# Earlier part closes, fewer expert steps in a B stage and more in a sort's end: one planner's order of a convolution with experts

## The chip, the cores and the metric

The kernel runs on one core of a Trainium2 chip. A core has TensorE (PE, with its weight loads shown as PEld), VectorE (DVE), ScalarE (ACT), GpSimd (POOL) and SyncE (SP), which issues the transfers. The time is device microseconds of one execution. Smaller is better.

## The reference

Two pieces follow each other. A long convolution along the sequence, through a Fourier transform of doubled length, and on its rows a layer of eight experts, of which each row uses the one with the highest logit:

```
x (8, 5696, 128), h (5696, 128)
Y = irfft(rfft(x, 2S) * rfft(h, 2S), 2S)[:, :S, :]        # S = 5696
r = Y.reshape(45568, 128)
logits = r @ w_gate                                        # (45568, 8)
e = argmax(logits);  gate = softmax(logits)[e]
out = gate * (relu(r @ w1[e]) @ w2[e])                     # w1 (8,128,1024), w2 (8,1024,128)
```

All of it is float32, and the output holds every row at its own place.

## The kernel before, in words

The doubled length is 2 x 48 x 119, so a transform goes in two factors. The eight batches are cut into groups of 2, 3 and 3 (`SPLIT`), numbered 0, 1 and 2, and each group passes three stages.

*Stage A* is the 119-point transform. Blocks of x are loaded (`xt`), split into two fp32r halves (`xc`, ScalarE L272 and another engine), multiplied (`pa`, L294), copied out (`ut`) and stored to `U` in DRAM (L287). For groups 1 and 2 it is a *guest* in the sort of the group before: `Guest.begin` puts two `pa` steps into each half-slot of that sort.

*Stage B* runs over the 120 frequencies of the first factor; an *item* is one of them for all batches of the group (in groups 1 and 2). An item is one 48-point product `xp` (L503, reads `uq`, loaded from `U` four frequencies at a time at L447, and `mt`), three multiplications with the filter's spectrum `hh` on VectorE (L515, L520, L522), a sum on GpSimd (L530), the inverse `vp` (L539) and a copy to `vt`, which is stored to `V` (L589).

*Stage C*, called the sort, takes `vq` back from `V`, makes the inverse 119-point product `yp` (L705), turns the rows (`tp`, L173), forms logits (`tp`, L746), counts rows by expert (`gb`, L770 and L771), works out every row's place, and GpSimd scatters each row to its expert's region of `SR` (L628). A slot is a pass over a few positions of all batches of the group: 16 slots in group 0 and 24 in groups 1 and 2, each of two half-slots, and each half-slot ends in a `yield`. When the slot named in `HALVES` is reached, a *part* closes: `tables` works out on VectorE (its last operations are the chain that ends at L948) which expert each tile of 256 rows belongs to, and after the last scatter of the part its rows may be loaded (`xr`, L1042).

*The experts.* 185 tiles of at most 256 rows are planned, cut by the parts into runs, and 182 of them are always computed. A tile is turned (`mx`, L173), passes layer 1 in four half-units (`mh`, L1091, six fp32r matmuls each), relu on ScalarE and VectorE (L1097, L1099), layer 2 in four half-units (`ma`, L1112), is copied (`ot`, L1122), turned back, scaled (`xr`, L1130) and scattered to the output (L1167). Weights come from `WD` in four pieces of 512 KB (`wb`, L1062); where the next tile has the same expert the load is skipped. Tiles done while a sort still scatters are staged in DRAM and scattered later.

*The order.* Each engine runs its instructions in the order written, SP's and GpSimd's queues too. That order comes from `run`: streams (the B and C stages in turn, the preparation of weights, the experts) are generators that yield a planned duration, and the stream with the least planned time goes next. An expert step is `STEP` = 1420 and holds one half-unit of layer 1 and one of layer 2. A B item of group 1 yields `STEP * MIX_B[1]` = 0.45 of a step, a half-slot of the sort `STEP * MIX_C[g]`, and half of that when all synthesis steps are done. `state["alone"]` is true while no part is ready; then no expert step goes beside the sort. `usable` lets a tile's rows be loaded `SETTLED` planned ns after the part's last scatter. After a sort's last half-slot the planner calls `next(after)`, which runs the next B stage's first loads.

Of the kernel before, what the change touches and what calls it, by code (L numbers as in the profile page):

```python
# [43 lines left out]
HALVES = ((12,), (8, 24), (24,))  # L44
STEP = 1420
MIX_A = (0.0, 0.45, 0.8)
MIX_B = (0.0, 0.45, 0.85)
MIX_C = (1.0, 1.2, 2.2)
STAGED = 64
# [3 lines left out]
HOLD = 3  # L53
GUESTED = (0,)
SETTLED = (2840, 8000, 8000)
# [12 lines left out]
def conv_moe(ctx: ExitStack, tc: tile.TileContext, I, out, B, S, D, E, F, split):  # L68
# [39 lines left out]
    class Part:  # L108
        def __init__(self, s, upto, tiles):
            self.s, self.upto, self.nt = s, upto, tiles  # L110
            self.sorted = self.tabled = self.filled = False
            self.lanes, self.fills = [], []
            self.since = 0
# [315 lines left out]
    def phase_b(gr, guest=None):  # L429
# [131 lines left out]
        N = len(items)  # L561
# [12 lines left out]
        for n in range(N + ds_ + 2 + HOLD):  # L574
# [28 lines left out]
            if n == N - 4 and g in GUESTED and guest:  # L603
                guest.fetch()
# [9 lines left out]
    state |= {"alone": True, "prepped": False, "defer": False, "spare": False, "now": 0}  # L614
# [43 lines left out]
    def phase_c(gr, guest=None, after=None):  # L658
# [9 lines left out]
        nu = NB // NI  # L668
# [194 lines left out]
        for k in range(AHEAD):  # L863
            divide(*divmod(k, nsub))
        TL, LL = TURN[g], LOGIT[g]
# [3 lines left out]
        for n in range(n_end + 1):  # L869
            for k in range(nsub):  # L870
# [17 lines left out]
                yield cost if n < nu else cost / 2  # L888
                if guest:
                    guest.end()  # L890
                if n < nu:
                    divide(*divmod(at + AHEAD, nsub))
                    settle(n, k)
# [19 lines left out]
        if guest:  # L913
            yield from guest.rest()
            state["spare"] = g > 0
        state["alone"] = False
        more = True
        while more or sorts:
            left = len(sorts)
            chore(3)  # L920
            more = after is not None and next(after, None)
            yield more or STEP
            if not more and len(sorts) == left:
                sort_one()
            if not sorts:
                state["defer"] = False
        chore(99)

    def tables(pt, base):
# [72 lines left out]
        pt.tabled = True  # L1002
# [179 lines left out]

    def usable(t):
        pt = seq[t][0]
        return pt.ready and state["prepped"] and not state["alone"] and state["now"] >= pt.since + SETTLED[min(pt.s, 2)]

    def pipeline(lo, hi):
# [3 lines left out]
        while True:  # L1191
            t, k = step
            while nw[0] < min(t + 3, hi) and seq[nw[0]][0].tabled and state["prepped"]:
# [18 lines left out]
            if act is None and old is None and to is None and ti is None:  # L1212
                leave(len(hist))
# [9 lines left out]
            if act:  # L1223
                layer1(t, k)
                passed[t, 0] = k
# [153 lines left out]
```

## Time and profile before

Three runs took 2313.42 to 2324.03 us, with a median of 2319.02 us.

| what | us |
|---|---|
| profiled execution, its own time | 2319.18 |
| its span | 2317.0 |
| TensorE busy | 2115.6 (91% of the span) |
| VectorE busy | 1556.2 (67%) |
| ScalarE busy | 1098.8 (47%) |
| GpSimd busy | 1193.0 (51%) |
| mean granted clock of TensorE | 0.966 |

Rows of the trace begin with the start in us from the beginning of the span, then the busy time of the row, the engine, the line of the code and the operation; out<-in are the program's names, and the bracket holds the idle time before it and what ended it ("issue": nothing that the profile shows). `SPq` is SP's own queue of transfers. A line by stretches gives, for each engine, its busy us and the number of instructions. A tile with name `xp`, `yp` or `mh` says which stage an instruction belongs to.

### The profile page before, as it was taken

Reading aid. Unit: us, or ns where it says so; the run is one execution under the profiler, and the core shown is the slowest. Engines: PE = TensorE matmul, PEld = TensorE weight load, DVE = VectorE, ACT = ScalarE, POOL = GpSimd, SP = SyncE. Lnnn points to the kernel's source line nnn. Section 1 sums busy time; section 2 is a strip of 40 time slices with the busy share of each in tenths; the row PEclk is TensorE's granted clock in tenths of the full one; section 3 lists DMA queues with packets and bytes.
Section 4 is the critical chain, followed back from the end, with each engine's and each line's share of the span. In section 5 each row is a group of like instructions: output and inputs, shape, how many; then the busy total and the mean of one; then the engine's idle time right before and its main releaser. Section 6 shows DMA issues by size and latency. Waiting matters only on the chain. (4 is left out here: it accounts for less than half of the span.)

```text
span 2317.0 us, 46736 instructions
## 1 busy us (share of the span) xinstructions
PE 2115.6 (91%) x14190; PEld 1776.5 (77%) x14190; DVE 1556.2 (67%) x3755; ACT 1098.8 (47%) x2359; POOL 1193.0 (51%) x1230
## 2 busy tenths in 40 slices
PE   7899787699997998978999999989879999999997
PEld 5688554366666887866777679878779999999997
DVE  4588644489996677768988785667565455555554
ACT  4688544233333665633434345556434444444443
POOL 5366337656653266752556561656554444444432
PEclk9999999799999999989999999999999999999998
DMA  9899998399997788857889877666645344444430
GB/s 294 272 323 319 317 341 236 118 262 284 268 276 217 204 257 255 235 160 214 235 243 261 225 234 212 191 176 194 176 130 157 129 136 138 137 137 136 140 116 28
DMA packets 254776, 485.47 MB, mean 210 GB/s; under 512 B 33221, under 2 KB 154690, under 8 KB 254523
## 3 DMA queue, kind: packets, MB, share of 16 engines
q1 hardware_dynamic: 230587, 435.36, 63.5%
q0 software_dynamic: 23936, 47.09, 6.6%
q8 instruction: 115, 1.88, 0.3%
q14 instruction: 138, 1.13, 0.2%
HBM read 592.96 MB, written 173.25 MB: 331 GB/s over the span
## 5 line engine op out<-in xcount | busy, mean ns | idle before, releaser
L1099 DVE SCALAR_TENSOR_TENSOR hs<-mh,hs 128x512 fp32r<-128x512 f32 x728 | 501.6, 690 | 451.7 <-ACT hs L1097 380.1
L1091 PE MATMUL mh<-xtb,wb 128*128 128x256 f32 x4368 | 708.5, 298 | 52.7 <-DMA wb<-WD 25.2
L1097 ACT ACTIVATE hs<-mh 128x512 fp32r<-128x512 f32 x728 | 434.5, 598 | 541.0 <-PE mh L1091 431.6
L1091 PEld LDWEIGHTS mh<-xtb,wb 128*128 128x128 f32 x4368 | 596.4, 193 | 122.4 <-issue 62.7
L1112 PE MATMUL ma<-hs,wb 128*128 128x256 f32 x4368 | 661.8, 288 | 7.5 <-DMA wb<-WD 5.7
L628 POOL DMA_INDIRECT SR<-rt,pi x384 | 404.2, 1053 | 380.1 <-ACT hs L1097 120.6
L1112 PEld LDWEIGHTS ma<-hs,wb 128*128 128x128 f32 x4368 | 580.6, 193 | 9.2 <-DMA wb<-WD 6.6
L1167 POOL DMA_INDIRECT out<-xr x256 | 250.2, 977 | 318.7 <-DVE xr L1130 272.8
L530 POOL TENSOR_TENSOR zt<-zt,xs 128x384 f32<-128x384 f32 (+1 forms) x280 | 297.4, 1071 | 122.2 <-DVE xs L522 92.7
L554 ACT COPY vt<-vp 96x384 f32<-96x384 f32 (+1 forms) x300 | 148.9, 496 | 348.1 <-PE vp L539 310.5
L539 PE MATMUL vp<-zt,mi 128*96 128x384 f32 (+1 forms) x720 | 259.0, 455 | 7.2 <-DVE xs L522 6.5
L503 PE MATMUL xp<-uq,mt 96*128 96x384 f32 (+1 forms) x720 | 259.9, 457 | 2.8 <-ACT vt L554 1.7
L515 DVE TENSOR_TENSOR zt<-xp,hh 128x384 f32<-128x384 f32 (+1 forms) x300 | 174.1, 580 | 57.5 <-PE xp L503 52.2
L294 PE MATMUL pa<-xc,fcr 120*120 120x512 f32 x576 | 170.6, 429 | 28.2 <-ACT xc L272 16.4
L1167 POOL DMA_INDIRECT out<-xb x108 | 105.6, 978 | 171.9 <-ACT ot L1122 108.4
L539 PEld LDWEIGHTS vp<-zt,mi 128*96 128x96 f32 x720 | 112.3, 163 | 102.8 <-issue 52.0
L522 DVE SCALAR_TENSOR_TENSOR xs<-xp,hh 64x384 f32<-64x384 f32 (+1 forms) x300 | 175.9, 586 | 6.0
L520 DVE TENSOR_TENSOR xs<-xp,hh 64x384 f32<-64x384 f32 (+1 forms) x300 | 173.3, 578 | 6.0
L294 PEld LDWEIGHTS pa<-xc,fcr 120*120 120x120 f32 x576 | 101.6, 191 | 67.3 <-ACT xc L272 18.0
L503 PEld LDWEIGHTS xp<-uq,mt 96*128 96x128 f32 x720 | 122.3, 193 | 32.5 <-issue 12.9
L307 DVE COPY ut<-pa 120x512 f32<-120x512 f32 x96 | 65.9, 687 | 108.1 <-PE pa L294 80.5
L705 PE MATMUL yp<-vr,gcr 120*120 120x384 f32 x576 | 118.1, 339 | 7.5 <-issue 3.0
(125 smaller groups left out, 2247.6 us busy)
## 6 DMA issues: line engine op xcount, KB each, us to landing
wb<-WD SPq DMA_DIRECT2D x728, 512.0 KB
vq<-V SPq DMA_DIRECT2D x64, 720.0 KB
U<-ut SPq DMA_DIRECT2D x48, 720.0 KB
uq<-U SPq DMA_DIRECT2D x60, 576.0 KB
V<-vt SPq DMA_DIRECT2D x60, 576.0 KB
xr<-SR SPq DMA_DIRECT2D x182, 130.0 KB
xt<-x SPq DMA_DIRECT2D x96, 240.0 KB
hh<-HS SPq DMA_DIRECT2D x120, 192.0 KB
```

The costliest lines, as they stand in the source:

```text
L294: nc.tensor.matmul(banks[m][:QN, :], lhs, rhs, start=(k == 0), stop=(k == len(ops) - 1))
L503: nc.tensor.matmul(xj, mt[:, k0 + j, :], uc.rearrange("p (b d) -> p b d", d=D), start=True, stop=True)
L515: nc.vector.tensor_tensor(out=zt, in0=x3, in1=hv[:, 0].broadcast_to([P] + wide), op=ALU.mult)
L522: nc.vector.scalar_tensor_tensor(out=xs[to], in0=x3[at], scalar=-1.0, in1=him, op0=ALU.mult, op1=ALU.mult)
L530: eng.tensor_tensor(out=zt, in0=zt, in1=xs, op=ALU.add)
L539: nc.tensor.matmul(vp[:K2, j * cw : (j + 1) * cw].rearrange("p (b d) -> p b d", d=D), mi[:, k0 + j, :], zt.rearrange("p b (j d) -> p b j d ...
L628: s = nc.gpsimd.indirect_dma_start(out=SR[:, :], out_offset=IndirectOffsetOnAxis(ap=pi[:, b : b + 1], axis=0), in_=rt[:, b, :], in_offset= ...
L1091: nc.tensor.matmul(hp[:, u, :], wb[:, a, f, :], xt[:, b, :], start=(n == 0), stop=(n == 2))
L1097: done = nc.scalar.activation(hs[:, 0], hp, AF.Relu)
L1099: nc.vector.scalar_tensor_tensor(out=hs[:, 1], in0=hp, scalar=0.0, in1=hs[:, 0].bitcast(F32), op0=ALU.max, op1=ALU.subtract)
L1112: nc.tensor.matmul(accs[t], wb[:, a, f, :], hs[:, b, u, :], start=(k == 0 and u == 0 and n == 0), stop=(k == NPAIR - 1 and u == 1 and n == 2),
L1167: sc = nc.gpsimd.indirect_dma_start(out=out[:, :], out_offset=IndirectOffsetOnAxis(ap=xr[:, s, D + 1 : D + 2].bitcast(I32), axis=0), in_=x ...
```

## The change

It changes numbers of the planner and adds four rules to it. No arithmetic is changed, and the same tiles, items and slots are computed.

- `HALVES`: part 0 closes at slot 10 (12 before) of group 0's 16, part 1 at slot 7 (8) of group 1's 24. Of the 185 planned tiles, part 0 holds 20 (26 before), part 1 37 (33), part 2 47 (45) and part 3 81 as before.
- `MIX_B[1]` 0.3 for 0.45: 3.33 B items of group 1 go to one expert step, where 2.22 went.
- `BESIDE` and `ENDING`: once experts run beside a sort, its half-slot yields 1.4, 1.2 or 2.2 steps by group as long as there is synthesis to do, and 1.4, 2.5 or 2.5 steps in its last ones, where it was half of `MIX_C`.
- `FETCHED`: the next group's first x blocks are loaded four items before the end of the B stage in group 1 too, not in group 0 alone.
- `EAGER`: in group 0's sort, from two slots before the end of the synthesis on, up to two of the next B stage's load steps are issued inside the sort, when the guest has ended at least four half-slots earlier. `guest.rest` runs only if the guest is not over.
- `KNOWN`: a weight load waits in the plan for 2840 planned ns after the tables.
- `acting`: in the loop behind a sort, a scatter of its own is issued whenever the experts issue no layer 1, also while `after` still has steps.

The diff:

```
@@ -41,17 +41,22 @@
 SHARES = (0.39, 0.93, 0.998, 0.84)
 AHEAD = 2
 ALONE = (0, 0, 20)
-HALVES = ((12,), (8, 24), (24,))
+HALVES = ((10,), (7, 24), (24,))
 STEP = 1420
 MIX_A = (0.0, 0.45, 0.8)
-MIX_B = (0.0, 0.45, 0.85)
+MIX_B = (0.0, 0.3, 0.85)
 MIX_C = (1.0, 1.2, 2.2)
+BESIDE = (1.4, 1.2, 2.2)
+ENDING = (1.4, 2.5, 2.5)
+KNOWN = 2840
 STAGED = 64
 PAIRED = 2
 HEAD = (0, 8, 8)
 EARLY = 2
 HOLD = 3
+FETCHED = (0, 1)
 GUESTED = (0,)
+EAGER = (2, 0)
 SETTLED = (2840, 8000, 8000)
 LEAD = (0, 4, 6)
 A3 = (True, True, True)
@@ -110,7 +115,7 @@
             self.s, self.upto, self.nt = s, upto, tiles
             self.sorted = self.tabled = self.filled = False
             self.lanes, self.fills = [], []
-            self.since = 0
+            self.since = self.known = 0
 
         @property
         def ready(self):
@@ -600,7 +605,7 @@
             if k0 == 0:
                 back_save(qb)
             drained = guest if n >= N and g in GUESTED else None
-            if n == N - 4 and g in GUESTED and guest:
+            if n == N - 4 and g in FETCHED and guest:
                 guest.fetch()
             if drained:
                 drained.begin(2)
@@ -611,7 +616,7 @@
     lanes = []
     state = {"w9": [const.tile([MP, max(SLOTS), E1], F32, name=f"w9{k}") for k in range(2)]}
     state["base"] = base0
-    state |= {"alone": True, "prepped": False, "defer": False, "spare": False, "now": 0}
+    state |= {"alone": True, "prepped": False, "defer": False, "spare": False, "now": 0, "acting": False}
 
     sorts, row = [], [0]
     scratch = fcs[:, 0]
@@ -862,6 +867,7 @@
             yield STEP * LEAD[g]
         for k in range(AHEAD):
             divide(*divmod(k, nsub))
+        finished, ahead = [None], [0]
         TL, LL = TURN[g], LOGIT[g]
         total_sub = nu * nsub
         sl = (LL + nsub - 1) // nsub + 1
@@ -885,9 +891,17 @@
                     score(n - sl, n - sl - 1)
                 if guest:
                     guest.begin(1 if k == 0 and n >= sl and not state["alone"] else 2)
-                yield cost if n < nu else cost / 2
+                if state["alone"]:
+                    yield cost if n < nu else cost / 2
+                else:
+                    yield STEP * (BESIDE if n < nu else ENDING)[g]
                 if guest:
                     guest.end()
+                    if guest.m >= guest.M and not guest.over and guest.done():
+                        finished[0] = at
+                if finished[0] is not None and at >= finished[0] + 4 and n >= nu - EAGER[g] and ahead[0] < 2:
+                    next(after)
+                    ahead[0] += 1
                 if n < nu:
                     divide(*divmod(at + AHEAD, nsub))
                     settle(n, k)
@@ -911,7 +925,8 @@
                 if at >= total_sub + LL:
                     break
         if guest:
-            yield from guest.rest()
+            if not guest.over:
+                yield from guest.rest()
             state["spare"] = g > 0
         state["alone"] = False
         more = True
@@ -920,7 +935,7 @@
             chore(3)
             more = after is not None and next(after, None)
             yield more or STEP
-            if not more and len(sorts) == left:
+            if len(sorts) == left and (not more or not state["acting"]):
                 sort_one()
             if not sorts:
                 state["defer"] = False
@@ -999,7 +1014,7 @@
             if prior is not None:
                 nc.vector.tensor_tensor(out=did, in0=did, in1=prior, op=ALU.add)
             state["done"] = did
-        pt.tabled = True
+        pt.tabled, pt.known = True, state["now"]
 
     def fill(pt, base):
         g = pt.s
@@ -1180,6 +1195,10 @@
             tc.add_manual_dep(sc, after.name, SYNC, reason="scatters are spread over the stage")
         outs.append(sc)
 
+    def known(t):
+        pt = seq[t][0]
+        return pt.tabled and state["prepped"] and state["now"] >= pt.known + KNOWN
+
     def usable(t):
         pt = seq[t][0]
         return pt.ready and state["prepped"] and not state["alone"] and state["now"] >= pt.since + SETTLED[min(pt.s, 2)]
@@ -1190,7 +1209,7 @@
         seen, hist, passed = {}, [None] * (LAG + 1), {}
         while True:
             t, k = step
-            while nw[0] < min(t + 3, hi) and seq[nw[0]][0].tabled and state["prepped"]:
+            while nw[0] < min(t + 3, hi) and known(nw[0]):
                 was, n = user[nw[0]], nw[1]
                 if home(nw[0]) and not state["spare"]:
                     break
@@ -1210,6 +1229,7 @@
             if ti is not None and (act and k < LAG or ti > t + 1 or act is None and ti > t):
                 ti = None
             if act is None and old is None and to is None and ti is None:
+                state["acting"] = False
                 leave(len(hist))
                 recall(len(hist))
                 deliver()
@@ -1222,6 +1242,7 @@
             recall(len(hist))
             if act:
                 layer1(t, k)
+                state["acting"] = True
                 passed[t, 0] = k
             if to is not None or ti is not None:
                 turn(to, ti)
```

Three places show the order. The first is TensorE at the end of group 0's sort. Before, the first rows are turned (`mxNone`) after all of the sort's matmuls (`gb0_16` is the last of them), and `mh0` follows at once:

```order
L173 MATMUL mxNone_0_4633<-ident_87,xr0_4549 128x128 x2
L1091 MATMUL mh0_0_4649<-xtb0_4646,wb0_0_4390 128x256 x6
L1091 MATMUL mh0_1_4663<-xtb0_4646,wb0_0_4390 128x256 x6
L1091 MATMUL mh0_2_4695<-xtb0_4646,wb0_1_4392 128x256 x6
L173 MATMUL mxNone_1_4702<-ident_87,xr1_4560 128x128 x2
L1112 MATMUL ma0_4705<-hs0_0_4656,wb0_2_4394 128x256 x6
```

In the change the same turn stands before the last slot's `yp0_15`, and `mh0` between its half-slots; `tp` are the turns and logits, `gb` the counts:

```order
L178 MATMUL mxNone_0_4419<-ident_87,xr0_4384 128x128 x2
L710 MATMUL yp0_15_0_4448<-vq0_15_4192,c_small_92 120x384 x2
L178 MATMUL tp0_15_0_4451<-ident_87,rt0_14_4321 128x120 x3
L751 MATMUL tp0_15_0_4451<-yt0_14_4434,c_small_92 32x120 x3
L775 LDWEIGHTS ones_94
L775 MATMUL gb0_13_4458<-oh0_12_4353,ones_94 128x54
L776 LDWEIGHTS c_small_92
L776 MATMUL gb0_13_4458<-oh0_12_4353,c_small_92 120x54
L178 MATMUL gb0_13_4458<-ident_87,lt0_13_0_4332 120x96
L178 MATMUL gb0_13_4458<-ident_87,lt0_13_1_4439 120x96
L1106 MATMUL mh0_0_4466<-xtb0_4463,wb0_0_4305 128x256 x6
L710 MATMUL yp0_15_1_4517<-vq0_15_4192,c_small_92 120x384 x2
```

What moved: the first turn and the first half-unit of tile 0 now stand ahead of the synthesis of slot 15, and that slot's matmuls and the last counts follow them.

The second place is SP's queue in the same stretch. Before, the loads of the first four tiles' rows (`xr0` to `xr3`) stand above these rows; then come the two last stores of `U` for group 1 (`ut1_11`), the first loads of the B stage (`mt`, `uq`, `mi`, `hh`), and the first weights:

```order
L287 DMA U1_72<-ut1_11_0_3956 120x1536
L287 DMA U1_72<-ut1_11_1_3958 120x1536
L439 DMA mt1_0_4638<-mq 96x512
L447 DMA uq1_0_4640<-U1_72 96x4x384
L450 DMA mi0_101<-miq 48x384 x2
L454 DMA hh0_98<-HS_76 48x2x512 x2
L1053 TENSOR_LOAD tab0_4354
L1053 ISA x2
L1054 TENSOR_LOAD tab0_4354
L1054 ISA x2
L1062 ISA
L1062 DMA wb0_0_4390<-WD_77 128x1024
```

In the change (the two stores of `ut1_11` and the loads of `vq0_15` and of `wb0_0` to `wb0_2` stand above these rows):

```order
L1077 DMA wb0_3_4311<-WD_77 128x1024
L444 DMA mt1_0_4313<-mq 96x512
L452 DMA uq1_0_4315<-U1_72 96x4x384
L455 DMA mi0_101<-miq 48x384 x2
L459 DMA hh0_98<-HS_76 48x2x512 x2
L1055 TENSOR_LOAD tab0_4180
L1055 ISA x2
L1057 ISA
L1057 DMA xr0_4384<-SR_69 128x260
```

What moved: the order was rows, `U` stores, B loads, weights; it is now `U` stores, weights, B loads, rows.

The third place is TensorE in the middle of group 1's B stage. Before, two or three items (`xp` with a `vp`) stand between expert steps (an `mh` with an `ma`):

```order
L503 MATMUL xp1_60_0_6470<-uq1_60_6335,mt1_60_6278 128x384
L539 MATMUL vp1_56_0_6472<-zt1_56_0_6387,mi2_103 96x384
L503 MATMUL xp1_61_0_6483<-uq1_60_6335,mt1_60_6278 128x384
L539 MATMUL vp1_57_0_6485<-zt1_57_0_6399,mi2_103 96x384
L1091 MATMUL mh8_3_6505<-xtb8_6258,wb0_1_4392 128x256 x6
L1112 MATMUL ma8_6445<-hs8_1_6405,wb0_2_4394 128x256 x6
L503 MATMUL xp1_62_0_6518<-uq1_60_6335,mt1_60_6278 128x384
L539 MATMUL vp1_58_0_6520<-zt1_58_0_6464,mi2_103 96x384
L503 MATMUL xp1_63_0_6536<-uq1_60_6335,mt1_60_6278 128x384
L539 MATMUL vp1_59_0_6538<-zt1_59_0_6475,mi2_103 96x384
L1091 MATMUL mh9_0_6566<-xtb9_6498,wb0_0_4390 128x256 x6
L1112 MATMUL ma8_6445<-hs8_2_6495,wb0_3_4396 128x256 x6
```

In the change three or four items stand between them:

```order
L508 MATMUL xp1_60_0_6247<-uq1_60_6103,mt1_60_6078 128x384
L544 MATMUL vp1_56_0_6249<-zt1_56_0_6188,mi2_103 96x384
L508 MATMUL xp1_61_0_6260<-uq1_60_6103,mt1_60_6078 128x384
L544 MATMUL vp1_57_0_6262<-zt1_57_0_6200,mi2_103 96x384
L508 MATMUL xp1_62_0_6272<-uq1_60_6103,mt1_60_6078 128x384
L544 MATMUL vp1_58_0_6274<-zt1_58_0_6218,mi2_103 96x384
L1106 MATMUL mh7_0_6302<-xtb7_6227,wb0_0_4305 128x256 x6
L1127 MATMUL ma6_6174<-hs6_2_6224,wb0_3_4311 128x256 x6
L508 MATMUL xp1_63_0_6322<-uq1_60_6103,mt1_60_6078 128x384
L544 MATMUL vp1_59_0_6324<-zt1_59_0_6252,mi2_103 96x384
L508 MATMUL xp1_64_0_6333<-uq1_64_6206,mt1_64_6181 128x384
L544 MATMUL vp1_60_0_6335<-zt1_60_0_6265,mi3_104 96x384
```

What moved: over the whole B stage 9.25 tiles stand between its first `xp` and its last `vp`, where 13.75 stood; the others are now behind the last `gb` of the third sort (95.5 tiles for 91.5) or in the sorts' ends.

More of the change, by code (lines that the diff above doesn't have):

```diff
@@ L53 @@
 HOLD = 3
+FETCHED = (0, 1)
 GUESTED = (0,)
+EAGER = (2, 0)
 SETTLED = (2840, 8000, 8000)
@@ L602, in phase_b @@
             drained = guest if n >= N and g in GUESTED else None
-            if n == N - 4 and g in GUESTED and guest:
+            if n == N - 4 and g in FETCHED and guest:
                 guest.fetch()
@@ L613, in conv_moe @@
     state["base"] = base0
-    state |= {"alone": True, "prepped": False, "defer": False, "spare": False, "now": 0}
+    state |= {"alone": True, "prepped": False, "defer": False, "spare": False, "now": 0, "acting": False}
     sorts, row = [], [0]
@@ L864, in phase_c @@
             divide(*divmod(k, nsub))
+        finished, ahead = [None], [0]
         TL, LL = TURN[g], LOGIT[g]
@@ L887, in phase_c @@
                     guest.begin(1 if k == 0 and n >= sl and not state["alone"] else 2)
-                yield cost if n < nu else cost / 2
+                if state["alone"]:
+                    yield cost if n < nu else cost / 2
+                else:
+                    yield STEP * (BESIDE if n < nu else ENDING)[g]
                 if guest:
                     guest.end()
+                    if guest.m >= guest.M and not guest.over and guest.done():
+                        finished[0] = at
+                if finished[0] is not None and at >= finished[0] + 4 and n >= nu - EAGER[g] and ahead[0] < 2:
+                    next(after)
+                    ahead[0] += 1
                 if n < nu:
@@ L913, in phase_c @@
         if guest:
-            yield from guest.rest()
+            if not guest.over:
+                yield from guest.rest()
             state["spare"] = g > 0
@@ L922, in phase_c @@
             yield more or STEP
-            if not more and len(sorts) == left:
+            if len(sorts) == left and (not more or not state["acting"]):
                 sort_one()
@@ L1001, in tables @@
             state["done"] = did
-        pt.tabled = True
+        pt.tabled, pt.known = True, state["now"]
     def fill(pt, base):
@@ L1181, in deliver, with known @@
         outs.append(sc)
+    def known(t):
+        pt = seq[t][0]
+        return pt.tabled and state["prepped"] and state["now"] >= pt.known + KNOWN
     def usable(t):
@@ L1192, in pipeline @@
             t, k = step
-            while nw[0] < min(t + 3, hi) and seq[nw[0]][0].tabled and state["prepped"]:
+            while nw[0] < min(t + 3, hi) and known(nw[0]):
                 was, n = user[nw[0]], nw[1]
```

11 lines of the change are left out of this document (8 added, 3 removed).

## The prediction

> **What bounds the kernel now.** I read the busy time by stretches first, then how many units of work each stretch holds, then the stalls of TensorE in order of time. A *tile* below is 256 expert rows: eight half-units (four mh, four ma) on TensorE. In order come the end of the first sort, the second group's B stage, the start of its sort, that sort, its end, and the tail of experts alone; the columns are length, PE, PEld, DVE, ACT, POOL busy, granted clock, DMA share and GB/s.
>
> ```profile
> span 2317.0 us, 46736 instructions
> ...
> 430.00:475.00 45.00, 26.70 (x148) 20.21 (x147) 21.15 (x109) 10.23 (x26) 24.53 (x30) 0.66 0.68 184
> 475.00:715.00 240.00, 235.14 (x1134) 156.33 (x1132) 231.40 (x423) 85.36 (x190) 150.35 (x153) 1.00 1.00 272
> ...
> 727.00:760.00 33.00, 21.98 (x145) 19.82 (x144) 13.35 (x23) 13.01 (x26) 1.96 (x2) 0.79 0.64 171
> 760.00:1000.00 240.00, 226.85 (x1643) 191.82 (x1642) 182.12 (x638) 149.46 (x349) 143.88 (x155) 0.99 0.83 241
> 1000.00:1048.00 48.00, 29.97 (x205) 27.49 (x204) 25.68 (x122) 11.67 (x29) 24.35 (x30) 0.82 0.58 157
> ...
> 1737.00:2290.00 553.00, 548.02 (x4547) 542.71 (x4547) 299.78 (x524) 257.73 (x525) 244.64 (x253) 0.99 0.40 131
> ```
>
> The tail is TensorE without a break. The B stage is different: VectorE is busy 231.4 of 240 us and the DMA engines have a share of 1.00, so TensorE's 235 busy us there hide slack. The ends of the sorts (430 to 475, 727 to 760, 1000 to 1048) leave TensorE idle for 11 to 18 us each, and its clock falls to 0.66, 0.79 and 0.82.
>
> The same stretches counted by one instruction per unit, first the copy that ends a tile (L1122), then one product per B item (L515):
>
> ```profile
> 475.00:727.00 252.00, 5.18 (x14) 1.00 0.99 270
> 1850.00:2250.00 400.00, 23.54 (x64) 1.00 0.41 136
> ...
> 475.00:727.00 252.00, 66.41 (x120) 1.00 0.99 270
> ```
>
> A tile alone costs 400/64 = 6.25 us. Now VectorE's groups from 500 to 700 us:
>
> ```profile
> L522 DVE SCALAR_TENSOR_TENSOR xs<-xp,hh 64x384 f32<-64x384 f32 x96 | 53.7, 560 | 1.7
> L515 DVE TENSOR_TENSOR zt<-xp,hh 128x384 f32<-128x384 f32 x96 | 53.1, 553 | 1.9 <-PE xp L503 0.3
> L520 DVE TENSOR_TENSOR xs<-xp,hh 64x384 f32<-64x384 f32 x96 | 52.9, 551 | 1.7
> L1099 DVE SCALAR_TENSOR_TENSOR hs<-mh,hs 128x512 fp32r<-128x512 f32 x44 | 30.4, 692 | 1.4
> L1130 DVE TENSOR_TENSOR xr<-mx,xr 128x256 f32<-128x256 f32 x11 | 4.6, 415 | 0.0
> L1082 DVE TENSOR_TENSOR xtb<-mx,xtb 128x256 fp32r<-128x256 f32 x11 | 4.6, 415 | 0.0
> ```
>
> A B item costs VectorE (53.7 + 53.1 + 52.9)/96 = 1.664 us, a tile (30.4 + 4.6 + 4.6)/11 = 3.6 us, and 96 items with 11 tiles make 199 of the 200 us. **So here a tile costs 3.6 us, not 6.25: work of experts is cheap inside the B stage.** That speaks against thinning it out there, which the change does.
>
> The stalls themselves, and the rows that part the program into segments:
>
> ```profile
> 429.18 2.27 PE L705 MATMUL yp<-vq,c_small 120*120 120x384 f32 x3 [3.34 <-issue]
> 448.75 0.69 PE L173 MATMUL mxNone<-ident,xr 128*128 128x128 f32 x2 [3.35 <-issue]
> 466.53 1.62 PE L1091 MATMUL mh<-xtb,wb 128*128 128x256 f32 x6 [9.55 <-DMA wb<-WD]
> 474.79 1.46 PE L503 MATMUL xp<-uq,mt 96*128 96x384 f32 x4
> 726.15 1.45 PE L539 MATMUL vp<-zt,mi 128*96 128x384 f32 x4
> 742.02 0.44 PE L705 MATMUL yp<-vr,gcr 120*120 120x384 f32 x1 [1.89 <-ACT vr L692]
> 752.73 3.21 PE L294 MATMUL pa<-xc,fcr 120*120 120x512 f32 x6 [8.58 <-ACT xc L272]
> 763.70 1.21 PE L705 MATMUL yp<-vr,gcr 120*120 120x384 f32 x6
> 1001.62 1.21 PE L705 MATMUL yp<-vr,gcr 120*120 120x384 f32 x6
> 1023.70 1.32 PE L1091 MATMUL mh<-xtb,wb 128*128 128x256 f32 x6 [4.60 <-DVE end L948]
> 1033.64 1.08 PE L1091 MATMUL mh<-xtb,wb 128*128 128x256 f32 x6 [3.49 <-DMA wb<-WD]
> 1046.41 1.62 PE L1091 MATMUL mh<-xtb,wb 128*128 128x256 f32 x6 [4.87 <-DMA wb<-WD]
> 1049.10 1.48 PE L503 MATMUL xp<-uq,mt 96*128 96x384 f32 x2
> 1693.52 1.21 PE L705 MATMUL yp<-vr,gcr 120*120 120x384 f32 x6
> 1712.29 0.27 PE L770 MATMUL gb<-oh,ones 120*128 120x54 bf16 x1
> ```
>
> **The change, segment by segment.** No instruction of weight is added; the same 182 tiles, items and slots stand in another order. So each segment is compared by its length and by the tiles that TensorE's order puts into it, counted from the order of both kernels.
>
> *First sort's end (to the first xp at 474.79).* The first rows can be loaded when the scatters of the closing slot have landed:
>
> ```profile
> 420.94 0.99 POOL L628 DMA_INDIRECT SR<-rt,pi  x1 [0.30 <-issue]
> ...
> 439.35 0.99 POOL L628 DMA_INDIRECT SR<-rt,pi  x1 [0.30 <-issue]
> ...
> 454.50 0.34 SPq L287 DMA_DIRECT2D U<-ut  x2
> 454.89 1.97 SPq L439 DMA_DIRECT2D mt<-mq  x1
> 461.37 0.32 SPq L447 DMA_DIRECT2D uq<-U  x1
> 466.30 0.12 SPq L1062 DMA_DIRECT2D wb<-WD  x1
> ```
>
> The row at 439.35 is the last scatter of slot 12, and TensorE turned the first rows 9.4 us later. Slot 10's last stands twelve scatters earlier, at 420.94, so the turn can come at 430.3, near the stalled yp at 429.18, and the sort's last slots then share TensorE with tiles. Left to do are 2.25 tiles (14.1 us; 1.75 before) and about 8 us of sort: the 26.7 us busy in the row from 430 to 475 at clock 0.66 are some 19 at full clock, less 1.75 tiles. The 9.55 us stall goes, because on SP's queue the last two U stores no longer wait behind the row loads; before, the load of uq waited 6.5 us for them (454.89 to 461.37) with the weight load at 466.30 behind it. To 22 us I add 5 for ten us at half clock and 3.5 for chain waits: xp at 461, **−14 us** (−20 if nothing waits, −5 if the row loads, now behind uq, mi and hh on SP, are late).
>
> The Trainium skill (TensorE: Matmul & The Clock Gate, What's actually happening) says the clock halves after an idle window of about 3.4 us and comes back after one as busy. The row at 0.66 agrees; by the rule a stall below that costs only itself, so this term would be nearer −17.
>
> *B stage (474.8 to 727.6, 252.8 us).* It held 13.75 tiles and holds 9.25: items come 3.33 instead of 2.22 to an expert step. By VectorE's prices before: 120 × 1.664 + 13.75 × 3.6 = 249.2, and 3.6 us of ramp; after: 199.7 + 33.3 + 3.6 = 236.6. The DMA share of 0.99 allows little more; I take 238, **−15** (−18 to 0, the last if the transfers already are the pace). The 4.5 tiles that leave turn up elsewhere at 6.25 us, which the last terms charge.
>
> The Trainium skill (DMA: Bandwidth & Descriptors, Specifications) puts the limit of a core's HBM traffic near 358 GB/s. The row shows 270 GB/s at a share of 0.99, so by the rule there is a third to spare and by the row none; by the rule the term is −16.
>
> *Start of the second sort (727.6 to 763.7, 36.1 us).* The next group's x blocks are fetched before the B stage ends, so the 8.58 us wait before pa goes, and most of the half clock behind it. What stays is the way from the last vp through the V store and the vq load to the first yp, 15 us, of which the order covers 1.75 tiles (10.9 us; 2 before). So a stall of about 4 us and 3.4 of half clock remain; with half a tile, two slots' halves and four pa (10 us) it is 28.5: **−7.5** (−11 to −2).
>
> *Second sort (763.7 to 1001.6).* One tile fewer (11.75 for 12.75): −6.25. But part 0 has only 20 tiles and runs dry earlier: four half-slots stand alone without an expert matmul, two before. What one alone costs:
>
> ```profile
> 907.49 1.31 PE L705 MATMUL yp<-vr,gcr 120*120 120x384 f32 x6 [0.82 <-issue]
> ...
> 912.58 1.31 PE L705 MATMUL yp<-vr,gcr 120*120 120x384 f32 x6 [0.24 <-ACT ut L307]
> ```
>
> 5.1 us, of which some 3.1 are TensorE's work: two more lose 4. **−2** (−6 to +6, with a clock drop).
>
> *Second sort's end (1001.6 to 1049.1, 47.5 us).* 3.5 tiles instead of 3, set 2.5 expert steps apart. The 3.49 us stall has the cause of 466.53 (weights behind a uq load that waits for U) and goes, as the U stores now stand two tiles earlier; the 4.60 (VectorE in the tables' chain) and the 4.87 (a change of expert) stay. 25 us were lost there; I take 17: 47.5 + 3.1 − 8.1, **−5** (−13 to +2).
>
> *Third group's B stage and sort.* 26 + 29.25 tiles for 26.25 + 29, same ratios: **0** (±4). *Its end (1693.5 to 1712.3, 18.8 us)* holds 2.25 tiles for 1.25, of which 5 us fill gaps: **+1** (−3 to +6). *The tail* takes 4 more tiles at 6.25: **+25**.
>
> Sum: −14 − 15 − 7.5 − 2 − 5 + 0 + 1 + 25 = −17.5. The profiled execution lasted 2319.2 us (2.2 around the span) and the median is 2319.0, so the forecast is **2302 us**, 0.75% faster. The tiles pushed into the tail eat more than the whole gain of the B stage; what is left comes from the sorts' ends.
>
> **The rivals.** (1) *Transfers set the pace.* For it: the share of 1.00 from 475 to 715; against: not one of VectorE's rows above waits for a DMA. The place is the B stage. Its bytes hardly shrink: 4.5 tiles' rows less, four x blocks more, some 3 us. Then B is −3, and the loads moved ahead of rows and weights queue too: first end −8, sort's start −3, sort's end 0, third B +4. With −2, +1 and +25 that is +14: 2333 us, slower. It decides from a B stage above 246 us. (2) *The ends stay as long*, because their stalls are chains and tables on VectorE, not lack of experts: −8 − 15 − 3 − 2 + 0 + 4 + 25 = +1: 2320. For it: 4.60 by L948; against: 9.55 and 8.58 are plainly queue order. (3) *The first rows come no earlier*, so the change does not do what it says: term one −3, total −6.5: 2313. Against: the scatters run back to back from 420.94. (4) *All terms at their good half*: −17 − 17 − 9 − 4 − 9 − 2 − 1 + 25 = −34: 2285.
>
> **How the numbers follow.** Forecast 0.48 (own range 2291 to 2312), transfers 0.17, ends stay 0.20, rows no earlier 0.06, all good 0.09. A measurement of this kernel tells 0.5%, 11.6 us, from no change. The forecast lies beyond that in nine tenths of its range: faster 0.43 + 0.09 = 0.52; same 0.05 + 0.20 + 0.06 = 0.31; slower 0.17. The range reaches into the first and the fourth rival: 2280 to 2331.
>
> **What would show it.** First xp of the B stage near 461 us and no stall above 5 us before it; B stage 235 to 241 us with VectorE above 95% (if it is 246 or more with VectorE idle, transfers rule); no wait of pa on xc at the second sort's start, but 3 to 5 us before its first yp; half-slots of 5 us in the middle of that sort; no wait for wb with uq ahead of it at its end; and 95 tiles, not 91, after the last gb at 6.2 us. I am wrong if the B stage does not shorten by at least 7 us, or if the first sort's end still holds a stall of 8 us.

## The result, and the profile after

The changed kernel took 2350.0 us (median of 2338.53 to 2354.64), the kernel before beside it 2316.35 us: a ratio of 1.0133, 95% interval 1.0087 to 1.0179. It is slower by 1.3%, where 0.75% faster was forecast. Its profiled execution lasted 2348.01 us around a span of 2346.2.

First the stretches of the changed kernel that answer to those shown of before (length, PE, PEld, DVE, ACT, POOL busy, granted clock, DMA share, GB/s): the first sort's end, the B stage, the second sort's start, its end, the way to the third sort, and the tail.

```profile
span 2346.2 us, 46767 instructions
...
430.00:461.40 31.40, 25.15 (x172) 21.37 (x173) 15.86 (x84) 10.52 (x26) 21.28 (x25) 0.81 0.43 113
461.40:700.00 238.60, 226.93 (x963) 135.34 (x962) 228.39 (x415) 79.51 (x175) 148.42 (x151) 1.00 1.01 273
700.00:735.00 35.00, 26.22 (x164) 24.12 (x162) 16.21 (x27) 14.96 (x29) 4.88 (x5) 0.85 0.79 218
...
973.00:1018.00 45.00, 30.36 (x224) 27.59 (x223) 21.88 (x98) 13.04 (x31) 21.88 (x27) 0.89 0.64 179
...
1350.00:1400.00 50.00, 42.41 (x286) 39.18 (x286) 24.55 (x44) 20.10 (x40) 16.83 (x18) 0.90 0.65 202
...
1730.00:2290.00 560.00, 550.85 (x4537) 545.30 (x4538) 299.52 (x529) 257.71 (x524) 243.61 (x252) 0.99 0.42 137
```

The first xp of the B stage now starts at 461.39 (474.79 before), and VectorE is busy for 228.39 of the B stage's 238.6 us. Up to there the forecast holds. The new thing is the row from 1350 to 1400, a clock of 0.90 at a place the prediction had put down as unchanged. A stretch of the same length around that place, in the kernel before:

```profile
1378.00:1428.00 50.00, 47.92 (x363) 44.02 (x361) 28.31 (x49) 25.67 (x52) 14.78 (x15) 1.00 0.80 254
```

Rows of TensorE there, from the last vp of the third B stage to the first yp of the third sort; first the changed kernel, then the one before:

```profile
1361.18 0.81 PE L544 MATMUL vp<-zt,mi 128*96 128x384 f32 x2
1375.89 0.95 PE L1106 MATMUL mh<-xtb,wb 128*128 128x256 f32 x6 [2.89 <-DMA wb<-WD]
1377.60 1.48 PE L1106 MATMUL mh<-xtb,wb 128*128 128x256 f32 x6
1384.97 1.62 PE L1106 MATMUL mh<-xtb,wb 128*128 128x256 f32 x6 [4.61 <-DMA wb<-WD]
1393.81 1.57 PE L710 MATMUL yp<-vr,gcr 120*120 120x384 f32 x6
```

```profile
1390.09 0.81 PE L539 MATMUL vp<-zt,mi 128*96 128x384 f32 x2
1392.22 0.44 PE L173 MATMUL mx<-ident,ot 128*128 128x128 f32 x2 [0.62 <-ACT ot L1122]
1412.07 1.62 PE L705 MATMUL yp<-vr,gcr 120*120 120x384 f32 x6
```

The same 3.25 tiles stand on this *way* in both orders, but it lasts 31.8 us instead of 21.2, with two waits for weights. Tile 57 is the first of part 2 in the changed kernel, and it stands here; before, part 2 began with tile 59, in the B stage. At this border a second set of weights comes into use, and eight pieces of 512 KB are issued in one run:

```profile
1380.40 10.81 SPq L1077 DMA_DIRECT2D wb<-WD  x8
```

Segment by segment, in us, each from the start of one named row to the next (a B stage ends with its last vp, and the tail begins at the third sort's last gb). The last column is the same difference on another chip (experiments 5 and 6), where the whole program takes less:

| segment | before | changed | moved | forecast | moved on the other chip |
|---|---|---|---|---|---|
| to the first xp of group 1 | 474.8 | 461.4 | −13.4 | −14 | −12.1 |
| B stage of group 1 | 252.8 | 239.5 | −13.3 | −15 | −13.2 |
| start of the second sort, to the yp of slot 1 | 36.1 | 32.3 | −3.8 | −7.5 | −2.6 |
| second sort | 237.9 | 240.1 | +2.2 | −2 | −3.9 |
| its end, to the first xp of group 2 | 47.5 | 44.8 | −2.7 | −5 | −3.6 |
| B stage of group 2 | 341.8 | 344.0 | +2.2 | 0 | +6.8 |
| way to the third sort | 21.2 | 31.8 | +10.6 | 0 | +9.7 |
| third sort | 281.5 | 293.0 | +11.5 | 0 | +1.5 |
| its end | 18.9 | 24.5 | +5.6 | +1 | +6.3 |
| tail | 604.7 | 635.0 | +30.3 | +25 | +25.1 |
| sum | | | +29.2 | −17.5 | +14.0 |

### The profile page after: what moved, and what is told of

The parts are those of the page before. It is cut to its first block, busy times and chain, and to the rows that moved or that the text cites. A ratio compares the mean times of both kernels' runs of the same rounds, so it can differ in the third digit from the quotient of the medians.

```text
span 2346.2 us, 46767 instructions
## 1 busy us (share of the span) xinstructions
PE 2130.3 (91%) x14190; PEld 1781.8 (76%) x14190; DVE 1557.8 (66%) x3755; ACT 1099.9 (47%) x2359; POOL 1190.8 (51%) x1230
## 5 line engine op out<-in xcount | busy, mean ns | idle before, releaser
L1127 PE MATMUL ma<-hs,wb 128*128 128x256 f32 x4368 | 667.1, 289 | 13.2 <-DMA wb<-WD 10.8
L299 PEld LDWEIGHTS pa<-xc,fcr 120*120 120x120 f32 x576 | 100.9, 190 | 61.3 <-ACT xc L277 11.2
```

What stands on the lines that cost most here:

```text
L299: nc.tensor.matmul(banks[m][:QN, :], lhs, rhs, start=(k == 0), stop=(k == len(ops) - 1))
L1127: nc.tensor.matmul(accs[t], wb[:, a, f, :], hs[:, b, u, :], start=(k == 0 and u == 0 and n == 0), stop=(k == NPAIR - 1 and u == 1 and n == 2),
```

## The experiments

Two theories stood against each other at first. **P (places):** an expert's weights are changed at fixed tiles; the change moves tiles and parts against the stages, and a change of part that falls on the way from a B stage to its sort, with nothing beside it, costs some 10 us. **R (rules):** the new rules themselves cost the third group its time. The times go by ratios to the kernel before on the same chip, which took 2238 to 2241 us for experiments 1 to 8 and 2315 to 2320 us for 9 to 16. *In front* below means tiles ahead of a row in TensorE's order.

**1. The new rules with the old numbers.**

```
-HALVES = ((10,), (7, 24), (24,))   +HALVES = ((12,), (8, 24), (24,))
-MIX_B = (0.0, 0.3, 0.85)           +MIX_B = (0.0, 0.45, 0.85)
```

> The changed kernel with HALVES and MIX_B of before; the other rules (BESIDE, ENDING, FETCHED, EAGER, KNOWN, acting) stay. Theory P (places): the third group lost time in the changed kernel because its tiles came 5 later there, so that the change from part 1 to part 2 (tile 57) fell on the third sort's start. Here 60.25 tiles stand before the last vp of the third B stage, as before, and tile 59 opens part 2 inside that stage. So from that vp to the first yp of the third sort about 21 us (21.2 before, 31.8 in the changed kernel), the third sort about 282 us (281.5 and 293.0), B stage of group 1 about 253 us with 13.75 tiles; the first xp near 465 us; 93.25 tiles behind the last gb; span near 2301 us. Theory R (the new rules themselves cost the third group its 24 us): start 31, third sort 293, span near 2325 us.

Ratio 0.9901 (0.9876 to 0.9926): faster. The way to the third sort took 20.2 us. So the rules don't lengthen it, R falls, and it is the two numbers that make the change slow.

**2. MIX_B alone, in the kernel before.**

```
-MIX_B = (0.0, 0.45, 0.85)   +MIX_B = (0.0, 0.3, 0.85)
```

> The kernel before with MIX_B[1] at 0.3 alone. B stage of group 1 near 239.5 us with 9.25 tiles, as in the changed kernel, and 98.5 tiles from the last gb on in the order (94.5 before). Theory P: part 2 opens with tile 59, and 59.25 tiles stand before the third sort's first yp, so the change of part falls on the way from the B stage to the sort again: 29 to 32 us there (21.2 before), and a span of 2336 to 2352 us. Theory R: none of the new rules is in it, so that way stays at 21 us, the third sort at 281, and the span is near 2332 us: 13 us gained in the B stage, 25 lost behind.

The B stage took 239.1 us, the way 28.4 (P's range was 29 to 32), the ratio is 1.0088 (1.0057 to 1.0118). Without any of the new rules the long way is there. The ratio alone tells little, since R expected a loss too, from the tail.

**3. MIX_B undone in the changed kernel** (0.45 for 0.3).

> The changed kernel with MIX_B[1] back at 0.45. 4.5 tiles more stand in the B stage of group 1 (13.75), 5 fewer in the second sort (6.75), where 21 half-slots then stand alone; everything behind is as in the changed kernel. Theory F (tiles in the second sort are free, since a half-slot alone lasts 5.1 us and one with its 0.25 tile as long): B stage +13, second sort still about 240 us, span near 2359 us. Theory W (a tile in the sort costs its 6.25 us of TensorE): second sort near 209 us, span near 2328 us. Part 2 opens with tile 57 and 58.25 tiles stand before the third sort's first yp, so the way there stays near 31.8 us by theory P.

Ratio 0.9978 (0.9961 to 0.9994); the way, with tile 57 on it, 30.1 us. The second sort took 210.6 us, and 225.5 with five tiles more (experiment 4, same chip and otherwise the same order there): a tile costs it 3.0 us, so neither F nor W holds. With the new rules, HALVES alone thus costs 0.8% against experiment 1 (0.9978 to 0.9901), and MIX_B alone 0.4% (experiment 7), where both cost 2.0% (experiment 6).

**4. The vq loads behind the weights.**

```
+        if g == 2:
+            yield STEP * 1
         for i in range(0 if guest and g == 0 else 2):
             load(i)
...
-            yield STEP * LEAD[g]
+            yield STEP * (LEAD[g] - (1 if g == 2 else 0))
```

> The changed kernel with the first two vq loads of the third sort issued one expert step later. TensorE's order is the same; on SP's queue the second and third weight pieces of tile 57 now stand ahead of these two loads, which wait for the last stores of V. Theory Q (the 4.61 us stall at 1385.0 is a weight piece behind the vq loads): that stall goes, the way from the last vp to the first yp is 27 us or less instead of 31.8, and the span about 5 us shorter. Rival: the change of part costs this wherever vq stands: still 31 to 32 us.

The way took 33.9 us, and the ratio is 1.0077 (1.0052 to 1.0103): Q is wrong. The second wait in tile 57 went and the first stayed, but tile 58, the first that uses the second set, then waited longer for its first piece:

```profile
1334.69 1.62 PE L1108 MATMUL mh<-xtb,wb 128*128 128x256 f32 x6 [2.30 <-DMA wb<-WD]
1350.51 1.62 PE L1108 MATMUL mh<-xtb,wb 128*128 128x256 f32 x6 [7.79 <-DMA wb<-WD]
```

So which load stands first doesn't decide it. That the amount does is likely, but no run changed the amount alone.

**5 and 6. Both kernels once more**, unchanged, for traces on one chip.

> The kernel before once more, for a trace on the same chip as the next three. Theory S: on the first chip ScalarE came some 2.5 us late in every second slot of the third sort (11 times before, 13 times in the changed kernel), on the chip of the first four experiments never; so where it doesn't, the third sort lasts 257 us, not 281. From the third B stage's last vp to the first yp 21 us.

> The changed kernel once more, timed beside the one before on this chip. Theory S: the third sort's 11.5 us more were ScalarE's lateness and not the order's, so where ScalarE is not late the third sort is within 2 us of the one before (257), and the ratio is 1.006 to 1.010. Theory P: the way from the last vp to the first yp stays 10 us longer (31 to 34 us against 21). Rival (the 11.5 us belong to the order): third sort near 268 us, ratio 1.013.

The way: 21.0 and 30.7 us, as P says. The third sort: 255.0 and 256.5 us, so S holds. The ratio is 1.0098 (1.0062 to 1.0133). The third sort of four profiles, as a stretch: the kernel before and the changed one of the first measurement, then of experiments 5 and 6.

```profile
1412.10:1693.50 281.40, 259.05 (x2114) 234.18 (x2113) 176.67 (x614) 150.34 (x356) 146.62 (x159) 1.00 0.65 185
```

```profile
1393.80:1686.80 293.00, 263.38 (x2131) 237.38 (x2130) 180.30 (x636) 152.88 (x364) 149.66 (x161) 1.00 0.60 168
```

```profile
1376.80:1631.90 255.10, 253.94 (x2115) 234.37 (x2114) 178.64 (x622) 151.33 (x360) 145.28 (x159) 1.00 0.72 204
```

```profile
1358.00:1614.40 256.40, 255.63 (x2130) 236.25 (x2129) 179.34 (x620) 152.32 (x362) 147.41 (x160) 1.00 0.69 190
```

TensorE idles for 22.3 and 29.6 us of the first two, for 1.2 and 0.8 us of the others, with the same order of work in it.

**7. HALVES undone in the changed kernel** (12, 8 and 24 for 10, 7 and 24).

> The changed kernel with HALVES of before and its own MIX_B of 0.3. 9.25 tiles in group 1's B stage, 13.5 in the second sort, 98 from the last gb on in the order (93.25 with both undone, 98.5 in the changed kernel). Tile 59 opens part 2, and 58.75 tiles stand before the third sort's first yp, so the change of part falls a quarter of a tile behind it. Theory P: against both undone 13 us gained in the B stage, 4.75 tiles by 6.5 us = 31 lost in the tail and 5 to 10 at the change of part: 23 to 28 us slower than both undone, ratio to before 1.000 to 1.003. Rival (tiles moved to the tail cost what they saved): ratio 0.990.

Ratio 0.9941 (0.9922 to 0.996), a miss on the good side. The way took 19.8 us, since tile 59 stands just behind it; the third sort took 262.9 us, 6 to 8 more than in experiments 5 and 6, with a wait for weights of 3.36 us at its start. The B stage is as expected (239.2 us), the tail 26 us longer than in the first experiment (617.9 for 591.8) where 31 was expected. The way to the first xp and the B stage of group 2 came out 10 us shorter together than there; executions of experiment 7 alone lie between 2220 and 2232 us, so one profile doesn't settle what that is. Against the changed kernel (1.0098 on this chip) HALVES cost 1.6%.

**8. The numbers turned the other way.**

```
+HALVES = ((13,), (7, 24), (24,))
+MIX_B = (0.0, 0.52, 0.85)
```

> The new rules with the numbers turned the other way: HALVES ((13,), (7, 24), (24,)) and MIX_B[1] 0.52, so that more expert tiles stand in group 1's B stage (15.88 for 13.75 with both undone) and fewer behind the last gb (91.5 for 93.25); only 0.12 tile stands before group 1's first xp. By the prices so far (some 2.4 us for a tile in that B stage, 6.5 in the tail): B stage +5, tail -11, first xp 0 to +4: 2 to 6 us faster than both undone, ratio to before 0.987 to 0.989. Rival (the later close of part 0 leaves TensorE idle at the first sort's end for what it wins): ratio 0.991 or more, first xp 6 us or more later.

Ratio 0.9934 (0.9906 to 0.9962): no gain over the first experiment. The first xp came no later (438.3 us against 439.6); the rival's ratio came about in another way: 2.1 more tiles made the B stage 10.0 us longer, 4.7 us a tile, the second sort took 238.1 us for 228.0, and the tail was 5 us shorter where 11 was expected.

**9. Part 1 of the changed kernel closes at slot 6.**

```
-HALVES = ((10,), (7, 24), (24,))   +HALVES = ((10,), (6, 24), (24,))
```

> The changed kernel with part 1 closing at slot 6 instead of 7. Part 2 then opens with tile 54, which stands 1.75 tiles ahead of the last vp of the third B stage, and not on the way to the third sort. Theory P (the change of part costs where no other work stands beside it): that way falls from 31 to 20 to 22 us, and the B stage grows by 3 us at most. The order holds 0.75 tile more up to the third sort's end, so the tail is 5 us shorter: in all 10 to 15 us faster than the changed kernel, ratio to before 1.003 to 1.005. Rival (the transition itself became longer by the new rules): still 30 us or more, ratio 1.007.

The way, with no wait on it, in the trace:

```profile
1357.28 0.81 PE L544 MATMUL vp<-zt,mi 128*96 128x384 f32 x2
1377.84 1.56 PE L710 MATMUL yp<-vr,gcr 120*120 120x384 f32 x6
```

19.8 us. The ratio is 0.9935 (0.9908 to 0.9962), so one slot turns 1.0 to 1.3% slower into 0.65% faster; that is better than P's range and more than the way explains. Against the changed kernel's profile the B stage of group 2 is 11.2 us shorter, the third sort 12.3 (see 5 and 6) and the tail 13.7, of which 0.75 tile is 5.

**10. MIX_B 0.33 for 0.3 in the changed kernel.**

> The changed kernel with MIX_B[1] 0.33 instead of 0.3. 12.25 tiles stand before the last vp of group 1's B stage (11.5), so the change of expert at tile 12 falls inside that stage, and not on the way to the second sort (15 comes behind it). Theory P: from the last vp to the first yp of slot 1 26 to 28 us, as with HALVES and MIX_B undone, instead of 33.5; the B stage 2 us longer; the rest as in the changed kernel (third sort's start still 31), ratio 1.007. Rival (these stalls come with the stage, whatever tile stands there): 33 us.

Ratio 1.0005 (0.9985 to 1.0025), better than the 1.007 expected. The start of the second sort took 22.0 us instead of 32.3. Its rows in the changed kernel, where tile 12 (a new expert) stands there, and then here, where it stands in the B stage:

```profile
700.12 0.81 PE L544 MATMUL vp<-zt,mi 128*96 128x384 f32 x2
703.62 0.96 PE L1106 MATMUL mh<-xtb,wb 128*128 128x256 f32 x6 [1.26 <-DMA wb<-WD]
709.03 0.95 PE L1106 MATMUL mh<-xtb,wb 128*128 128x256 f32 x6 [2.31 <-DMA wb<-WD]
711.29 1.49 PE L1127 MATMUL ma<-hs,wb 128*128 128x256 f32 x6 [0.87 <-DMA wb<-WD]
720.25 1.65 PE L1127 MATMUL ma<-hs,wb 128*128 128x256 f32 x6 [4.34 <-DMA wb<-WD]
...
733.16 1.21 PE L710 MATMUL yp<-vr,gcr 120*120 120x384 f32 x6
```

```profile
713.19 0.89 PE L544 MATMUL vp<-zt,mi 128*96 128x384 f32 x2 [0.19 <-POOL zt L535]
726.47 0.34 PE L710 MATMUL yp<-vr,gcr 120*120 120x384 f32 x1
727.35 1.13 PE L710 MATMUL yp<-vr,gcr 120*120 120x384 f32 x5 [0.54 <-DVE vr L698]
731.92 1.22 PE L710 MATMUL yp<-vr,gcr 120*120 120x384 f32 x6
736.08 1.21 PE L710 MATMUL yp<-vr,gcr 120*120 120x384 f32 x6
```

The waits for wb are gone. The way to the third sort, with tile 57 still on it, took 33.5 us.

**11. EAGER undone, with the old numbers** (both entries set to −99).

> HALVES and MIX_B undone as in the first experiment, and EAGER too: group 1's first loads come only behind the first sort. The order then has 2.75 tiles before the first xp (0.75), 5.5 at the second sort's end (3.5), and 91 from the last gb on (93.25). If EAGER's gain is the earlier first xp: that comes 10 to 14 us later (near 451), the tail is 15 us shorter, the second sort's end 8 to 12 us longer: ratio 0.990 to 0.993, so EAGER is worth next to nothing. Rival (EAGER is what made the new rules win): first xp 16 us later or more, ratio 0.996 or more.

Ratio 0.9923 (0.9899 to 0.9947), inside the first range; but the first xp came at 474.9 us, 19 later than with EAGER on such a chip (456.0, experiment 16), as the rival said. The tail (585.1 us for 596.5) gives most of it back. By ratios EAGER is worth 0.5% against experiment 16 and 0.2% against experiment 1, which is within the noise.

**12. BESIDE and ENDING undone, with the old numbers.**

```
-BESIDE = (1.4, 1.2, 2.2)   +BESIDE = (1.0, 1.2, 2.2)
-ENDING = (1.4, 2.5, 2.5)   +ENDING = (0.5, 0.6, 1.1)
```

> HALVES and MIX_B undone, and BESIDE and ENDING too (1.0, 1.2, 2.2 and half of that in the last steps). The order has 0 tiles before group 1's first xp, 1 at the second sort's end (3.5), and 97.75 from the last gb on (93.25); 60.25 tiles stand before the third sort's first yp, and tile 59 opens part 2, on the way there. Theory P: tail +29, the two sorts' ends -9 and -6, third sort's start +10: 20 to 27 us slower than with HALVES and MIX_B undone alone, ratio 1.000 to 1.003. Rival (the ends are bound by chains, and tiles in them come free, so that without them the ends stay as long): ratio 1.006 or more.

Ratio 0.997 (0.9943 to 0.9997), a little better than P's range. The way, with tile 59 on it, took 32.2 us. The second sort's end took 19.5 (40.7 in experiment 16), so the ends don't stay as long, and the tail 629.3 (596.5).

**13. The kernel before, with the border moved onto the way.**

```
-HALVES = ((12,), (8, 24), (24,))   +HALVES = ((12,), (9, 24), (24,))
```

> The kernel before with one number changed: part 1 closes at slot 9 instead of 8. Part 2 then opens with tile 62, and 59.75 tiles stand before the last vp of the third B stage and 63 before the third sort's first yp: the change of part is moved onto that way, and no new rule is in the kernel. Theory P: the way grows from 21 to 29 to 33 us; 0.5 tile more in the tail is 3 us; ratio 1.004 to 1.006. Rival (the new rules are needed for the loss): 21 us, ratio 1.001.

```profile
1381.02 0.81 PE L539 MATMUL vp<-zt,mi 128*96 128x384 f32 x2
1383.62 0.98 PE L1091 MATMUL mh<-xtb,wb 128*128 128x256 f32 x6 [0.36 <-DVE hs L1099]
1395.97 0.95 PE L1091 MATMUL mh<-xtb,wb 128*128 128x256 f32 x6 [1.19 <-DMA wb<-WD]
1405.99 1.62 PE L1091 MATMUL mh<-xtb,wb 128*128 128x256 f32 x6 [6.92 <-DMA wb<-WD]
1412.65 1.55 PE L705 MATMUL yp<-vr,gcr 120*120 120x384 f32 x6
```

30.8 us instead of 21.2, with the wait for wb, and a ratio of 1.0068 (1.0046 to 1.009), a little more than expected. One number, none of the new rules, and the kernel before has the long way.

**14. Both changes moved off** (the changed kernel with slot 6 and MIX_B 0.33).

> The changed kernel with MIX_B[1] 0.33 and part 1 closing at slot 6: tile 12's change of expert lies inside group 1's B stage, and tile 54 opens part 2 inside the third. Theory P: from the last vp to the yp of slot 1 of the second sort 22 to 24 us (32.3 in the changed kernel), to the first yp of the third 19 to 21 us (31.8), B stage of group 1 near 241.5; ratio 0.989 to 0.992, below slot 6 alone (0.9935). Rival (what is won at one place is lost at the next): ratio 0.993 or more.

The two starts took 25.8 (2 more than expected) and 19.8 us, the B stage 241.1, and the ratio is 0.9887 (0.9866 to 0.9909): better than either alone (0.9935 and 1.0005). Against the changed kernel (1.0098 in experiment 6) the two gain 1.6% and 0.9% alone and 2.1% together, so most of it adds up.

**15 and 16. The best order found, and the first experiment again.**

```
+HALVES = ((12,), (6, 24), (24,))
+MIX_B = (0.0, 0.47, 0.85)
```

> The new rules with HALVES ((12,), (6, 24), (24,)) and MIX_B[1] 0.47. 14.5 tiles in group 1's B stage, no change of expert from 15.25 to 17.25 tiles (the second sort's start) nor from 61 to 64.25 (the third's), 92.5 tiles from the last gb on (93.25 in the next run). Against the next run: second sort's start -4 us, tail -5, B stage +2.5: 3 to 8 us faster. Rival (tile 32's change, now in the second sort's end, takes it back): equal.

> The first experiment once more (new rules, HALVES and MIX_B of before), beside the others on one chip: ratio 0.988 to 0.993; from the last vp to the first yp of the third sort 20 us.

Ratio 0.9812 (0.9787 to 0.9836) and 0.9875 (0.9854 to 0.9895, just under its range): the new rules with these numbers beat both kernels, by 1.9% and by about 3%. Against 16 the second sort's start took 24.2 us for 25.7, and the tail 588.1 for 596.5; the profiles differ by 11 us, somewhat more than the 3 to 8 expected.

The way to the third sort, over all runs, with the border of parts as TensorE's order has it:

| border | runs | way, us |
|---|---|---|
| in the B stage ahead | before, 1, 5, 8, 9, 11, 14, 15, 16 | 18.9 to 22.2 |
| just behind the way | 7 | 19.8 |
| on the way | changed, 2, 3, 4, 6, 10, 12, 13 | 28.4 to 33.9 |

## Why the prediction was wrong

**What held.** The first rows' turn came ahead of the last slots, and the 9.55 us wait behind U's stores went: −13.4 for −14. The B stage follows VectorE's prices: 239.5 us, forecast 238, at a DMA share of 1.01; the transfers' rival, which needed 246 us, is out. The wait of pa on xc is gone. But by its letter one sign of being wrong was met, a stall of 8 us at the first sort's end: TensorE idles until the first rows can be turned.

```profile
431.65 0.66 PE L178 MATMUL mxNone<-ident,xr 128*128 128x128 f32 x2 [8.18 <-issue]
```

Most of this wait lies before 430.3, where the forecast's sum for that segment begins, so the length came out all the same. Four more tiles in the tail cost 25.1 us on the chip of experiments 5 and 6; of the 30.3 in the first measurement, 5 are not explained by a run.

**The step that failed** is "Third group's B stage and sort … same ratios: **0** (±4)". I counted how many tiles stand in each segment, and not which. The ratios are the same, but the third group begins 5 tiles earlier in the row of tiles, and part 2 two tiles earlier, so that its first tile came to stand on the way to the sort: +10.6 us. Experiments 9 and 13 show this cause from both sides. No rival had it. With the B stage (+2.2) and the sort (+11.5) this term came to +24.3 us, and to +18.0 on the other chip.

**Start of the second sort: −7.5 forecast, −3.8 measured.** The same omission once more. With the x blocks fetched and no new expert there it takes 22.0 to 25.8 us (10, 14, 15), which would have been a gain of 10 to 14; tile 12's change took most of it. A smaller part also has its changes closer together: 20 tiles for eight experts, where there were 26. The stall of about 4 us that the prediction kept there did come (4.34 us), but as a wait for weights, not for V: that is luck.

**Third sort: +11.5.** 4.3 us are more work of TensorE (263.4 for 259.1; a quarter of a tile is 1.6) and 7.3 more idle time (29.6 for 22.3). The late starts of ScalarE, told of in the last section, add up to 33.7 us in this sort for 25.7 before, which goes with the idle time. On the chip of experiments 5 and 6, with none of them, the same two orders differ by 1.5 us. So it is not the order alone; why this trace lost more than the third sorts of experiments 9 to 16 on chips of the slower kind (274 to 282 us) isn't settled.

**Its end: +1 forecast, +5.6.** The tile added there costs its 6.25 us; I had let 5 of them fill gaps, and none was filled.

**Second sort and its end** came out 4 and 2 us worse than forecast in the first measurement, and 2 us better and 1 worse in the other pair; two pairs of single executions don't settle it. At that end one wait for weights is left, 6.45 us, where 3.49 and 4.87 stood:

```profile
1015.33 1.62 PE L1106 MATMUL mh<-xtb,wb 128*128 128x256 f32 x6 [6.45 <-DMA wb<-WD]
```

The sum −17.5 thus lacked 10.6 and 4 for changes of weights, 11.5 for the third sort, some 5 at its end and 5 in the tail; 11 more are small differences in the other segments. By ratios the two numbers of the change cost about 2% (0.9901 to 1.0098), and its rules win 1%: the prediction saw both, but priced the numbers only by tiles. Its sentence against thinning out the B stage pointed the right way; it should have carried the sign.

The Trainium skill (TensorE: Matmul & The Clock Gate, What's actually happening) puts the window after which the clock halves near 3.4 us. The traces show steps of that length, but shorter waits were enough here. Two steps of the changed kernel, the first with the wait of 2.89 us in it:

```profile
1373.69:1377.10 3.41, 1.21 (x10) 1.24 (x11) 0.00 (x0) 0.23 (x1) 0.97 (x1) 1.00 0.89 287
1377.10:1380.51 3.41, 3.27 (x16) 2.97 (x15) 1.38 (x2) 1.07 (x3) 0.52 (x1) 0.50 1.02 258
```

The mh right behind that wait still took 0.95 us, the next one 1.48. Behind 2.31 us it is 0.95 and then, after 0.87 us more of waiting, 1.49; in experiment 4 the mh behind 2.30 us took 1.62 at once. Behind the 1.19 us of experiment 13 it took 0.95, and the clock stayed at 1.00. So what the prediction drew from that rule, that a shorter stall costs only itself, doesn't hold here. An uncovered change of weights costs its wait and, in most of these rows, the half clock besides.

## What to carry to other kernels

When an edit shifts work against a schedule, count not only how many units stand in each segment but which ones: those that bring a reload with them (a new expert, a new part, a second buffer) are cheap beside other work and cost some 10 us here where a stage changes. Where a planner's numbers are tuned, look at where these units fall after each step; a neighbouring number that moves them by one or two can be worth more than the edit: here 1.6 to 2% for one slot, of which the border on the way explains 12 us, 0.5%. And work taken out of a segment is a gain only if the place it goes to costs less: a tile cost 3 us in group 1's B stage (4.7 when more were put in) and in the second sort, and 6.3 in the tail.

## What the runs showed of the hardware

The same program differs between chips by more than any edit here: the kernel before took 2238 to 2241 us on two chips (experiments 1 to 8) and 2315 to 2320 us in the first measurement and in experiments 9 to 16. Single instructions take as long on both kinds: in the third sort of the changed kernel and of experiment 4, VectorE's hs takes 687 and 688 ns and a matmul of yp 337 and 337. What makes the two kinds differ, no run tested. Part of it is ScalarE starting late: in the changed kernel of the first measurement, the relu of a half-unit that ends at about 1511.0 starts 3 us later,

```profile
1510.07 0.95 PE L1106 MATMUL mh<-xtb,wb 128*128 128x256 f32 x6
```

```profile
1508.25 0.37 ACT L1137 COPY ot<-ma 128x256 f32<-128x256 f32 x1
1514.09 0.60 ACT L1112 ACTIVATE hs<-mh 128x512 fp32r<-128x512 f32 x1 [5.46 <-PE ma L1127]
```

and in experiment 6, at the same place of the order, 0.1 us after it:

```profile
1467.18 0.95 PE L1106 MATMUL mh<-xtb,wb 128*128 128x256 f32 x6
```

```profile
1465.70 0.38 ACT L1137 COPY ot<-ma 128x256 f32<-128x256 f32 x1
1468.23 0.60 ACT L1112 ACTIVATE hs<-mh 128x512 fp32r<-128x512 f32 x1 [2.15 <-PE mh L1106]
```

Delays of over 1 us of this kind are 15 and 20 in the two first profiles, 17 to 23 in experiments 9 to 16, most of them in the sorts and their ends, and none in experiments 1 to 8. In the third sorts they add up to 25.7 and 33.7 us in the two first profiles and to 18 to 31 in experiments 9 to 16, where TensorE idles 15 to 22 us.

ScalarE itself isn't what is late. It waits for a semaphore that TensorE raises, and the trace has the times of these: for the row at 1514.09 it rose at 1514.00, 3.0 us after the half-unit's end as the profile models it, and for the first time since 1509.28. In 184 of the 185 delays of these ten profiles ScalarE starts within 0.25 us of such a signal. Some of the signals are missing on these chips (2094 of 2335 are on record in the changed kernel, 2330 in experiment 6). Whether TensorE's matmuls end late there or only its signals, the traces don't show, and no run tested it.
